# The last projection, the gate and one block of w2 change their places in the stream of a decode block

## The chip, the core and the metric

The kernel runs on one core of one Trainium2 chip. The metric is the device time of one execution in microseconds (us). Before the change it is 1055.42 us, the median of 3 runs (1055.36 to 1056.06). Smaller is better.

## The reference, cut to what matters

One token of one sequence passes through an attention with a long cache and a feed-forward part; a conditioning vector c gives six vectors that shift, scale and gate both. All is float32: D = 640, 32 heads of 192, 8192 cached positions, F = 1536.

```python
mod = (_silu(c) @ w_mod).reshape(c.shape[0], 6, 1, -1)
sa, ca, ga, sb, cb, gb = (mod[:, 0], mod[:, 1], mod[:, 2], mod[:, 3], mod[:, 4], mod[:, 5])
h = _layernorm(x, axis=-1) * (1 + ca) + sa
x = x + ga * _A_ref(h, A_k_cache, A_v_cache, A_wq, A_wo)      # softmax(q k / sqrt(192)) v, then @ wo
h = _layernorm(x, axis=-1) * (1 + cb) + sb
x = x + gb * _B_ref(h, B_w1, B_b1, B_w2, B_b2)                # relu(h w1 + b1)^2 w2 + b2
```

The two caches are 403 MB and the weights some 49 MB; each byte is used once.

## The kernel before, in words

**The stream.** All that comes from HBM is laid out by the host in the order of its use. It comes as `wm0`, 53 chunks (0 to 52) of `kv`, `wm1`, `w1`, `w2`, each with the 128 partitions as rows. All transfers are issued by SyncE (`load`, L197 to L211) and go through one queue. They land in three buffers of 16128 columns that take turns (tag "slot"): `load(n + 3)` stands at the end of the work on chunk n (L401) and waits until the buffer of chunk n is no longer read. The last chunk, `wm1`, `w1` and `w2` come in pieces, so that work can start on the first columns: the tuples `WM_CUT`, `W1_CUT`, `W2_CUT` (L43 to L45) hold the columns where a piece ends.

**A chunk** holds keys, values and, in some, a part of the query or output weights. `plan()` (L50) lays this out: (first key row, key rows, first value unit, value units, extras), an extra being ("o", pair of heads) with 1920 columns or ("q", part) with 2560. The last two chunks hold values alone. Chunk 51 holds 9 units of values and the output weights of pair 14; chunk 52 holds 7 units, in two pieces of four and three. The output weights of the last pair, 15, come at the head of `wm1`.

**Work on a chunk** (loop of L354): VectorE multiplies keys with the query (`multiply`, L249), GpSimd adds two halves of a part of the products (L376), VectorE sums (`scores`, L257), and at the end of a head the softmax follows (L268). TensorE multiplies the values (`values`, L298). After a pair of heads, `evict` (L303) and `turn` (L318) bring its output into a column, and `attend` (L324) multiplies that with the pair's part of wo and accumulates over all pairs in `att_a`.

**The end** (from L403), in program order: evict, turn and `attend` of the last pair; `mod(2, 3)`, three of the six conditioning vectors from `wm1`, with `gather` (L338) between, which brings the attention into `att_s` and spreads it; x1, layernorm, `hT2`; `gate(5)` (L424), the last conditioning vector, whose weights are the first 3200 columns of `w1`; the products with w1 (`ps_f`, L428); bias, relu and square on VectorE, then a transposition to `fT` (L431 to L434); one idle product that keeps TensorE warm (L438); the products with the 12 blocks of w2 (`ps_y`, L446); `y` and its transfer out (L451). Each engine works through its instructions in this order and waits where an operand is missing.

Of the kernel before, what the change touches and what calls it, by code (L numbers as in the profile page):

```python
# [8 lines left out]
F32 = mybir.dt.float32  # L9
# [4 lines left out]
P = 128  # L14
D = 640
H = 32
SK = 8192
DH = 192
FF = 1536
G = 4  # L20
DG = D // G
FG = FF // G
KB = DG // 32
FB = FG // 32
# [4 lines left out]
NPAIR = H // 2  # L29
NPOS = SK // P  # L30
POOL = 7
WO = 3 * D
QC = 512
NQ = H * DH // QC
RING = 3 * QC
SRING = 4 * NPOS
WQ = KB * QC
UNIT = E * DH
SLOT = 84 * DH
VPC = 5  # L40
LEAD_FROM = 1300
LEAD = 120
W1_CUT = (KB * D + 3 * FF, KB * D + KB * FF)  # L43
W2_CUT = (8 * D, 11 * D, 12 * D)
WM_CUT = (WO + 9 * D, WO + 15 * D)  # L45
WARM = 1
# [3 lines left out]
def plan():  # L50

    chunks, kp, vp, q, o = [], 0, 0, 1, 0
    while kp < H * NPOS or vp < H * NPOS // E:
        room, w = SLOT, []
        if o < NPAIR - 1 and 2 * (o + 1) * NPOS // E <= vp:
            w.append(("o", o))
            o, room = o + 1, room - WO
        used = (QC * (q - 2) - 1) // DH + 1 if q > 2 else 0
        if q < NQ and kp >= NPOS * (QC * q // DH) - 3 * NPOS // 2 and kp >= NPOS * used:
            w.append(("q", q))  # L60
            q, room = q + 1, room - WQ
        if not chunks:
            nk, nv = NPOS, 0
        else:
            v = VPC - 1 if kp >= LEAD_FROM else VPC
            nk = min(H * NPOS - kp, (room - v * UNIT) // DH)
            if kp + nk - E * (vp + v) > LEAD:
                v += 1
                nk = min(H * NPOS - kp, (room - v * UNIT) // DH)
            nv = min(H * NPOS // E - vp, (room - nk * DH) // UNIT)  # L70
            while nv and ((vp + nv - 1) // (NPOS // E) + 1) * NPOS > kp + nk:
                nv -= 1
            nk = min(H * NPOS - kp, (room - nv * UNIT) // DH)
        chunks.append((kp, nk, vp, nv, w))
        kp, vp = kp + nk, vp + nv
    assert q == NQ and o == NPAIR - 1
    return chunks


def width(chunk):  # L80
    return chunk[1] * DH + chunk[3] * UNIT + sum(WO if t == "o" else WQ for t, _ in chunk[4])


PLAN = plan()


@with_exitstack
def block_kernel(ctx: ExitStack, tc: tile.TileContext, kv, wm0, wm1, w1, w2, out):
    nc = tc.nc
    const = ctx.enter_context(tc.tile_pool(name="const", bufs=1))  # L90
# [102 lines left out]

    chunk_t = {}
    start = [sum(width(c) for c in PLAN[:n]) * P for n in range(len(PLAN))]

# [26 lines left out]
    h1 = layernorm(x_c, 1, scale_a, lambda: ma[:, :KB, 0], "ln1")  # L223
    qb = const.tile([P, RING], F32, name="qb")

# [8 lines left out]
    att_a = psum.tile([P, 512], F32, tag="att", name="att_a")  # L234
    att_s = const.tile([P, D], F32, name="att_s")
    nc.vector.memset(att_s, 0.0)
    query(0, wm0_t[:, KB * 2 * D:KB * 2 * D + WQ])
# [100 lines left out]
    def gather():  # L338

        nc.vector.tensor_copy(att_s[96:, :512], att_a[96:, :512])  # L340
        for j in range(NV):
            r = slice(32 * j, 32 * (j + 1))
            nc.scalar.activation(att_s[r, 512:], att_a[r, (D - 512) * j:(D - 512) * (j + 1)], AF.Copy)
        att_t.append(psum.tile([P, 512], F32, tag="o", name="att", bufs=3))
        for g in range(G):
            nc.tensor.matmul(att_t[0][32 * g:32 * (g + 1), :DG], sel.to_broadcast([P, 32]),
                             att_s[:, DG * g:DG * (g + 1)], start=True, stop=True)
# [6 lines left out]
    for n, (kp, nk, vp, nv, extra) in enumerate(PLAN):  # L354
# [5 lines left out]
        for what, k in extra:  # L360
            w = t[:, at:at + (WO if what == "o" else WQ)]
            at += w.shape[1]
            if what == "q":
                query(k, w)
            else:
                wo_t = (k, w)
# [29 lines left out]
        for v in range(vp, vp + nv):  # L396
            if v % (NPOS // E) == NPOS // E - 1:
                to_evict.append(v // (NPOS // E))
        if wo_t is not None:
            attend(*wo_t)  # L400
        load(n + 3)  # L401

    wm1_t, w1_t, w2_t = chunk_t["wm1_t"], chunk_t["w1_t"], chunk_t["w2_t"]  # L403
    gb_t = w1_t[:, :KB * D].rearrange("p (b n) -> p b n", b=KB)
    w1_t = w1_t[:, KB * D:KB * (FF + D)].rearrange("p (b n) -> p b n", b=KB)
    w2_t = w2_t[:, :FB * D].rearrange("p (b n) -> p b n", b=FB)

    for h in to_evict:
        evict(h)
    turn(NPAIR - 1)  # L410
    attend(NPAIR - 1, wm1_t[:, :WO])
    mod(2, 3, wm1_t[:, WO:WO + KB * 3 * D].rearrange("p (b n) -> p b n", b=KB), gather)
    x1 = const.tile([P, DG], F32, name="x1")
# [9 lines left out]

    gate(5, gb_t)  # L424
    pf = psum.tile([P, 512], F32, tag="q", name="ps_f", bufs=2)
# [8 lines left out]
    fT = columns(f, FG, "fT", work, tag="om", bufs=1)  # L434

    idle = psum.tile([P, 512], F32, tag="sm", name="ps_warm", bufs=2)
    for k in range(WARM):
# [6 lines left out]
    for b in range(FB):  # L444
        for g in range(G):
            nc.tensor.matmul(py[32 * g:32 * (g + 1), :DG], fT[:, b], w2_t[:, b, DG * g:DG * (g + 1)],  # L446
                             start=(b == 0), stop=(b == FB - 1))
# [46 lines left out]
```

## Time and profile before

| | us |
|---|---|
| median of 3 runs | 1055.42 |
| the profiled execution's own time | 1055.57 |
| its span, first to last instruction | 1053.8 |
| VectorE busy | 830.2 |
| TensorE busy (products) | 495.8 |
| GpSimd busy | 188.1 |

The span is what the profile shows; the execution's own time has 1.8 us more around it. Positions such as 1036.71 are us from the start of the span. In rows of the timeline stand the start, the duration, the engine, the line of the kernel, the operation, the tiles written and read with their shapes, the count, and in brackets the idle time before and who ended it. SPq is SyncE's queue, on which a row of a transfer is its issue; the rows of the transfers give size and us from issue to landing. Rows of a chain of waits give start, duration, what. Rows of stretches give the stretch and its length, for PE, PEld, DVE, ACT and POOL the busy us and in brackets the instructions, and then three numbers: the granted clock of TensorE (1.00 is full), the busy share of the 16 DMA engines, and GB/s.

### The profile page before, as it was taken

The page shows a single profiled execution, that of the slowest core. Times are in us where ns is not written, and L with a number is a line of the kernel's source. Part 1 is how long each engine was busy: PE and PEld are TensorE (multiplying, and loading weights), DVE is VectorE, ACT ScalarE, POOL GpSimd, SP SyncE. Part 2 cuts the span into 40 slices and gives each one's busy share as a digit, 9 for nine tenths or more (in the row PEclk, how much of TensorE's full clock was granted, in tenths as well). Part 3 has the DMA queues.
Part 4 walks back from the last instruction along what each step waited for, and adds up shares of the span by engine and source line. Part 5 has one row for each costly group of instructions (what it writes and reads, how often), then busy time and mean ns, then how long its engine had stood idle before and what let it go on. Part 6 is the DMA issues. An engine that isn't in the chain of part 4 may idle for free.

```text
span 1053.8 us, 5121 instructions
## 1 busy us (share of the span) xinstructions
PE 495.8 (47%) x2102; PEld 134.6 (13%) x2102; DVE 830.2 (79%) x428; ACT 43.4 (4%) x122; POOL 188.1 (18%) x57
## 2 busy tenths in 40 slices
PE   2153335455352363536344357344446346345286
PEld 1010011011010010101011011011011011011023
DVE  2898878877959969887797895999887977988822
ACT  1000000000000000000000000000000000000001
POOL 0212121121212202212121121122211211211200
PEclk9676576777675686668676577676777767768699
DMA  9999999999999999999999999999999999999997
GB/s 408 434 429 431 429 441 438 441 431 433 430 431 431 432 433 430 433 435 438 435 427 436 433 427 430 436 439 433 431 432 431 432 436 433 437 433 430 419 431 311
DMA packets 8959, 452.15 MB, mean 429 GB/s; under 512 B 996, under 2 KB 1000, under 8 KB 1256
## 3 DMA queue, kind: packets, MB, share of 16 engines
q1 hardware_dynamic: 8936, 451.83, 99.3%
q8 instruction: 16, 0.26, 0.1%
q14 instruction: 7, 0.06, 0.0%
HBM read 451.82 MB, written 0.00 MB: 429 GB/s over the span
## 4 chain that ended last, share of the span: by engine, by line
DMA 56%; DVE 31%; PE 11%; ACT 1%; issue 0%; SPq 0%; DVEq 0%
DMA chunk<-in_kv 53%; DVE chunk L249 16%; DVE sc L257 13%; PE ps_o L298 5%; DMA w_t<-in_w 2%; PE ps_q L230 2%; PE att_a L331 2%; DMA wm_t<-in_wm 1%; DVE os L312 1%; DVE om L310 1%; ACT p L281 0%; PE ps_mod L179 0%; PE ps_mx L273 0%; PE ps_mod L188 0%; PE att_a L333 0%
## 5 line engine op out<-in xcount | busy, mean ns | idle before, releaser
L249 DVE TENSOR_TENSOR chunk<-chunk,qb 128x8064 f32<-128x8064 f32 (+19 forms) x81 | 419.7, 5211 | 128.4 <-DMA chunk<-in_kv 123.2
L257 DVE TENSOR_REDUCE sc<-chunk 128x25 f32<-128x4800 f32 (+21 forms) x109 | 333.9, 3097 | 0.4
L298 PE MATMUL ps_o<-chunk,p 128*32 128x512 f32 x1536 | 296.7, 736 | 73.7 <-DMA chunk<-in_kv 64.3
L376 POOL TENSOR_TENSOR chunk<-chunk 128x1824 f32<-128x1824 f32 (+9 forms) x51 | 187.4, 3674 | 806.3 <-DVE chunk L249 548.4
L273 PE MATMUL ps_mx<-ident,mp 128*128 128x128 f32 x32 | 14.6, 455 | 343.9 <-DVE mp L271 343.9
L298 PEld LDWEIGHTS ps_o<-chunk,p 128*32 128x32 f32 x1536 | 67.4, 131 | 278.1 <-issue 188.1
L331 PE MATMUL att_a<-chunk,oT 128*32 128x512 f32 x90 | 63.4, 863 | 42.2 <-DVE oT L321 42.2
L230 PE MATMUL ps_q<-chunk,ln_h 128*128 128x512 f32 x110 | 66.9, 769 | 26.1 <-DMA chunk<-in_kv 26.1
L273 PEld LDWEIGHTS ps_mx<-ident,mp 128*128 128x128 f32 x32 | 5.6, 176 | 373.0 <-DVE mp L271 304.0
L281 ACT ACTIVATE p<-sc,nm 128x256 f32<-128x256 f32 x32 | 16.2, 507 | 649.9 <-DVE nm L275 649.9
L230 PEld LDWEIGHTS ps_q<-chunk,ln_h 128*128 128x128 f32 x110 | 26.5, 252 | 64.5 <-issue 35.1
L310 DVE TENSOR_TENSOR om<-ps_o,mask 96x512 f32<-96x512 f32 x32 | 21.6, 675 | 8.5 <-PE ps_o L298 8.5
L275 DVE TENSOR_REDUCE nm<-ps_mx 128x1 f32<-128x128 f32 x32 | 9.3, 292 | 19.5 <-PE ps_mx L273 19.5
L312 DVE TENSOR_REDUCE os<-om 96x64 f32<-96x512 f32 x32 | 21.8, 682 | 1.1
L331 PEld LDWEIGHTS att_a<-chunk,oT 128*32 128x32 f32 x90 | 11.7, 145 | 77.4 <-DVE oT L321 44.4
L320 DVE TENSOR_REDUCE oT<-ps_oT 128x3 f32<-128x96 f32 x16 | 4.0, 248 | 20.3 <-PE ps_oT L316 20.3
L286 PE MATMUL ps_sum<-ident,wide 128*128 128x128 f32 x16 | 7.5, 467 | 22.4 <-ACT wide L284 22.4
L179 PE MATMUL ps_mod<-wm_t,silu 128*32 128x320 f32 (+1 forms) x80 | 9.2, 608 | 15.5 <-DVE silu L167 15.5
L316 PE MATMUL ps_oT<-ident,os 96*128 96x96 f32 x16 | 5.0, 313 | 22.3 <-DVE os L312 22.3
L333 PE MATMUL att_a<-chunk,oW 128*96 128x384 f32 x30 | 14.1, 550 | 0.0
L231 ACT ACTIVATE qb<-ps_q 128x512 f32<-128x512 f32 x12 | 7.2, 597 | 136.7 <-PE ps_q L230 136.7
L329 ACT ACTIVATE oW<-oT 128x96 f32<-128x96 f32 x16 | 4.5, 280 | 177.5 <-DVE oT L321 177.5
(84 smaller groups left out, 100.9 us busy)
## 6 DMA issues: line engine op xcount, KB each, us to landing
chunk<-in_kv SPq DMA_DIRECT2D x38, 8064.0 KB, 37.5
chunk<-in_kv SPq DMA_DIRECT2D x11, 8000.0 KB, 38.3
chunk<-in_kv SPq DMA_DIRECT2D x2, 7872.0 KB, 38.5
chunk<-in_kv SPq DMA_DIRECT2D x1, 6144.0 KB, 27.6
wm_t<-in_wm SPq DMA_DIRECT2D x1, 4493.5 KB, 13.6
w_t<-in_w SPq DMA_DIRECT2D x1, 3904.0 KB, 20.7
wm_t<-in_wm SPq DMA_DIRECT2D x1, 3840.0 KB, 23.8
chunk<-in_kv SPq DMA_DIRECT2D x1, 3072.0 KB, 28.2
```

What stands on the lines that cost most here:

```text
L230: nc.tensor.matmul(ps, h1[:, b:b + 1].to_broadcast([P, P]), w[:, b], start=(b == 0), stop=(b == KB - 1))
L249: nc.vector.tensor_mul(pr, pr, q[:, None, :].to_broadcast([P, b - a, DH]))
L257: nc.vector.tensor_reduce(sc[:, a % SRING:a % SRING + b - a], src[:, a - first:b - first], axis=AX.X, op=ALU.add)
L273: nc.tensor.transpose(ps[:, :P], mp.to_broadcast([P, P]), ident)
L275: nc.vector.tensor_reduce(nm, ps[:, :P], axis=AX.X, op=ALU.max, negate=True)
L281: nc.scalar.activation(p, s[:, :, None].to_broadcast([P, NPOS, 32 // E]), AF.Exp, bias=nm, accum_out=sp[:, h % 2:h % 2 + 1])
L298: nc.tensor.matmul(ps_t[h][32 * g:32 * (g + 1)], p[:, E * j:E * (j + 1)].rearrange("p e r -> p (e r)"), t[:, g], start=(j == 0), stop=last)
L310: nc.vector.tensor_mul(om[:n], ps_t.pop(h)[:n].rearrange("p (d e) -> p d e", e=E), mask[:n, None, :].to_broadcast([n, ED, E]))
L312: nc.vector.tensor_reduce(os_[:n, h % 2], om[:n], axis=AX.X, op=ALU.add)
L331: nc.tensor.matmul(att_a[96:, :512], oT[:, j:j + 1].to_broadcast([P, 32]), w[:, j, :512], start=(first and j == 0), stop=(last and j == NV ...
L333: nc.tensor.matmul(att_a[:96, :NV * (D - 512)], oW.rearrange("p j r -> p (j r)"), w[:, :, 512:], start=first, stop=last)
L376: nc.gpsimd.tensor_add(half, half, kt[:, m:, DH // 2:])
```

## The change

The last pair's output weights go to the end of chunk 52 (its second piece), and `wm1` holds the conditioning weights alone. In `w1` the weights of the feed-forward part come first and the gate's after them, and `gate(5)` moves from before the w1 products to after `fT`. The first of the 12 blocks of w2 leaves the last transfers: it has an array `w2x` and a tile `w2x_t` of its own, and comes in two transfers, rows 0 to 124 behind the issue of chunk 23 and rows 125 to 127 behind that of chunk 24. The rest of w2 has pieces that end at columns 7 D, 11 D - 160 and 11 D. `att_s` shares the buffer of `qb`, and its memset goes from VectorE at the start to GpSimd at the end.

```diff
+EXTRA = {"o": WO, "q": WQ}
...
-W1_CUT = (KB * D + 3 * FF, KB * D + KB * FF)
-W2_CUT = (8 * D, 11 * D, 12 * D)
-WM_CUT = (WO + 9 * D, WO + 15 * D)
+W1_CUT = (3 * FF, KB * FF + KB * D)
+W2_CUT = (7 * D, 11 * D - DG, 11 * D)
+FIVE = {20: (0, 125), 21: (125, P)}
+WM_CUT = (9 * D, 15 * D)
...
     assert q == NQ and o == NPAIR - 1
+    chunks[-1][4].append(("o", NPAIR - 1))
     return chunks
...
+    w2x_t = const.tile([P, D], F32, name="w2x_t")
...
-    qb = const.tile([P, RING], F32, name="qb")
+    qb = work.tile([P, RING], F32, name="qb", tag="qb", bufs=1)
...
-    att_s = const.tile([P, D], F32, name="att_s")
-    nc.vector.memset(att_s, 0.0)
...
     def gather():
 
+        att_s = work.tile([P, D], F32, name="att_s", tag="qb", bufs=1)
+        nc.gpsimd.memset(att_s, 0.0)
...
-        if wo_t is not None:
+        if wo_t is not None and n + 1 < len(PLAN):
             attend(*wo_t)
         load(n + 3)
+        if n in FIVE:
+            a, b = FIVE[n]
+            nc.sync.dma_start(w2x_t[a:b], w2x[a:b])
...
-    gb_t = w1_t[:, :KB * D].rearrange("p (b n) -> p b n", b=KB)
-    w1_t = w1_t[:, KB * D:KB * (FF + D)].rearrange("p (b n) -> p b n", b=KB)
-    w2_t = w2_t[:, :FB * D].rearrange("p (b n) -> p b n", b=FB)
+    gb_t = w1_t[:, KB * FF:KB * (FF + D)].rearrange("p (b n) -> p b n", b=KB)
+    w1_t = w1_t[:, :KB * FF].rearrange("p (b n) -> p b n", b=KB)
+    w2_t = w2_t[:, :(FB - 1) * D].rearrange("p (b n) -> p b n", b=FB - 1)
...
     turn(NPAIR - 1)
-    attend(NPAIR - 1, wm1_t[:, :WO])
-    mod(2, 3, wm1_t[:, WO:WO + KB * 3 * D].rearrange("p (b n) -> p b n", b=KB), gather)
+    attend(*wo_t)
+    mod(2, 3, wm1_t[:, :KB * 3 * D].rearrange("p (b n) -> p b n", b=KB), gather)
...
-    gate(5, gb_t)
     pf = psum.tile([P, 512], F32, tag="q", name="ps_f", bufs=2)
...
     fT = columns(f, FG, "fT", work, tag="om", bufs=1)
 
+    gate(5, gb_t)
     idle = psum.tile([P, 512], F32, tag="sm", name="ps_warm", bufs=2)
...
-            nc.tensor.matmul(py[32 * g:32 * (g + 1), :DG], fT[:, b], w2_t[:, b, DG * g:DG * (g + 1)],
+            nc.tensor.matmul(py[32 * g:32 * (g + 1), :DG], fT[:, b], (w2_t[:, b - 1] if b else w2x_t)[:, DG * g:DG * (g + 1)],
                              start=(b == 0), stop=(b == FB - 1))
```

More of the change, by code (lines that the diff above doesn't have):

```diff
@@ L76, in plan, with block_kernel @@
     assert q == NQ and o == NPAIR - 1
+    chunks[-1][4].append(("o", NPAIR - 1))
     return chunks
 def width(chunk):
-    return chunk[1] * DH + chunk[3] * UNIT + sum(WO if t == "o" else WQ for t, _ in chunk[4])
+    return chunk[1] * DH + chunk[3] * UNIT + sum(EXTRA[t] for t, _ in chunk[4])
 PLAN = plan()
 @with_exitstack
-def block_kernel(ctx: ExitStack, tc: tile.TileContext, kv, wm0, wm1, w1, w2, out):
+def block_kernel(ctx: ExitStack, tc: tile.TileContext, kv, wm0, wm1, w1, w2, w2x, out):
     nc = tc.nc
@@ L476 @@
     kv = [np.concatenate([k[:, kp:kp + nk].reshape(P, -1), v[:, vp:vp + nv].reshape(P, -1)]
-                         + [(wo if what == "o" else wq)[i] for what, i in extra], axis=1).reshape(-1)
+                         + [{"o": wo, "q": wq}[what][i] for what, i in extra], axis=1).reshape(-1)
           for kp, nk, vp, nv, extra in PLAN]
@@ L482 @@
                                column(B_b1, FB), column(B_b2, KB)], axis=1),
-        "wm1": np.concatenate([wo[-1], rows(wm[:, 2 * D:5 * D], KB)], axis=1),
-        "w1": np.concatenate([rows(wm[:, 5 * D:], KB), rows(B_w1, KB)], axis=1),
-        "w2": rows(B_w2, FB),
+        "wm1": rows(wm[:, 2 * D:5 * D], KB),
+        "w1": np.concatenate([rows(B_w1, KB), rows(wm[:, 5 * D:], KB)], axis=1),
+        "w2": rows(B_w2, FB)[:, D:],
+        "w2x": rows(B_w2, FB)[:, :D],
     }
```

2 lines of the change are left out of this document (1 added, 1 removed).

## The prediction

> **What bounds the kernel now.** I read the page first, then the chain of waits for the last 115 us, then the timeline of the end, then stretches of the transfer rates and of the clock.
>
> ```profile
> span 1053.8 us, 5121 instructions
> PE 495.8 (47%) x2102; PEld 134.6 (13%) x2102; DVE 830.2 (79%) x428; ACT 43.4 (4%) x122; POOL 188.1 (18%) x57
> HBM read 451.82 MB, written 0.00 MB: 429 GB/s over the span
> L249 DVE TENSOR_TENSOR chunk<-chunk,qb 128x8064 f32<-128x8064 f32 (+19 forms) x81 | 419.7, 5211 | 128.4 <-DMA chunk<-in_kv 123.2
> chunk<-in_kv SPq DMA_DIRECT2D x38, 8064.0 KB, 37.5
> ```
>
> No engine is full, and VectorE waits 123 us for chunks: the stream from HBM bounds the body. A chunk of 8064 KB (8.26 MB) needs 19 us at 429 GB/s, and lands 37.5 us after its issue, so one more is always queued ahead of it. The end is another matter; the chain shows it.
>
> ```profile
> 943.04 39.25 DMA chunk<-in_kv
> 982.32 8.56 DVE chunk L249
> ...
> 1015.98 20.69 DMA w_t<-in_w
> 1036.71 4.43 PE ps_mod L188 x20
> ...
> 1046.98 3.50 PE ps_y L446 x96
> 1050.51 0.34 DVE y L449
> ```
>
> The reader is to see two anchors. The last chunk with keys lands at 982.32, and from there everything is computed work. Then the gate's weights (first piece of w1) land at 1036.71 and TensorE runs gate, w1, w2 with one break, in which VectorE makes f. Beside that chain stands the timeline:
>
> ```profile
> 982.32 8.56 DVE L249 TENSOR_TENSOR chunk<-chunk,qb 128x8064 f32<-128x8064 f32 x1 [1.36 <-DMA chunk<-in_kv]
> 1015.88 6.21 PE L298 MATMUL ps_o<-chunk,p 128*32 128x512 f32 x42
> 1024.59 2.76 PE L331 MATMUL att_a<-wm_t,oT 128*32 128x512 f32 x6 [0.68 <-DVE oT L321]
> 1027.28 0.89 PE L333 MATMUL att_a<-wm_t,oW 128*96 128x384 f32 x2
> 1037.75 0.34 DVE L122 STREAM_TRANSPOSE hT<-ln_h 128x160 f32<-128x160 f32 x1
> 1041.07 3.43 PE L428 MATMUL ps_f<-w_t,hT 128*32 128x384 f32 x40
> 1041.19 1.21 ACT L192 ACTIVATE mods<-ps_mod 32x160 f32<-32x160 f32 x4 [4.58 <-PE ps_mod L188]
> 1044.43 1.12 PE L438 MATMUL ps_warm<-w_t,ones 128*128 128x512 f32 x2
> 1046.98 3.47 PE L446 MATMUL ps_y<-w_t,fT 128*32 128x160 f32 x96 [1.43 <-DVE gb L440]
> ```
>
> hT2 is ready at 1037.75 + 0.34 = 1038.09, but TensorE is in the gate until 1041.07: the w1 products start 2.98 us late. That is what the new order can give back.
>
> **The change, part by part.** First the block of w2. The end of the stream says why a moved block isn't neutral: its share falls in a step.
>
> ```profile
> 1044.50:1045.50 1.00, 1.00 (x2) 0.22 (x2) 0.90 (x2) 0.00 (x0) 0.00 (x0) 1.00 0.81 330
> 1045.50:1046.50 1.00, 0.05 (x1) 0.00 (x0) 0.93 (x3) 0.00 (x0) 0.00 (x0) 1.00 0.59 241
> 1046.50:1047.50 1.00, 0.52 (x16) 0.55 (x20) 0.76 (x3) 0.00 (x0) 0.00 (x0) 1.00 0.52 215
> 1047.50:1048.50 1.00, 1.00 (x37) 1.00 (x32) 0.00 (x0) 0.00 (x0) 0.00 (x0) 1.00 0.48 178
> 1048.50:1049.50 1.00, 1.00 (x39) 1.00 (x32) 0.00 (x0) 0.00 (x0) 0.00 (x0) 1.00 0.10 38
> w_t<-in_w SPq DMA_DIRECT2D x1, 320.0 KB, 26.6
> 1015.98 7.44 SPq L210 DMA_DIRECT2D w_t<-in_w  x5
> ```
>
> From 1045.5 to 1048.5 the share stands near a half: about eight of the 16 DMA engines are done by 1045.3, the others work on to 1048.6. Every transfer so far gives each engine the same bytes, so I estimate that eight engines lead by 3.3 us.
>
> 125 rows can be dealt out evenly over at most 5 of 16 engines (125 = 5 x 25), 3 rows over 3. One engine runs at 178 / (0.48 x 16) = 23 to 215 / (0.52 x 16) = 26 GB/s in these rows. 25 rows of 2560 bytes are 64,000 bytes: 2.5 to 2.8 us more on five engines, in mid-stream, and nothing on the others; one of the 3 rows adds 0.1. The removed block, 320 KB over 16, was 20,480 bytes on each, 0.8 us at the very end. The Trainium skill, DMA: Bandwidth & Descriptors, section "Why a DMA increments its semaphore by 16 and not by 1", has the same dealing (the largest count up to 16 that divides the rows, on HWDGE the lowest-numbered engines), and its table of rules advises one 128-partition transfer. By that advice the block would best have stayed 0.8 us on every engine; by the step above the late ones have no time to spare and the early ones do.
>
> If the five are early ones, 3.3 - 2.7 = 0.6 us of their lead remains: no landing comes later, and the last ends at 1048.6 - 0.8 = 1047.8 instead of 1048.6. **That gain is worth nothing here**: the five issues end at 1023.42, so the last began at about 1023.0 and landed 26.6 us later, at 1049.6, and TensorE reaches its columns at about 1050.2 (the last 8 of 96 matmuls before 1046.98 + 3.47 = 1050.45). If the five are late ones, every later landing, that of 982.32 too, slips by 2.7 us. The trace has no row on who is who; the bounds are 0 and 2.7. The nearest row is the step itself: it stays flat for three us, so these are two groups and not a spread, and five neighbours are likely to lie in one of them. Which one is a judgement: I take 0, at odds of better than 2 to 1, and keep 2.7 in the range. [...]
>
> SyncE issues two transfers more behind the issues of chunks 23 and 24, at about 0.4 us; no issue waits on them, as chunks are queued 18 us ahead. Nothing waits for w2x_t before ps_y.
>
> **The last wo** moves from the head of wm1 to the tail of chunk 52. It has the same place in the byte order, but the second piece of the chunk now lands with it, 1920 columns (983,040 bytes, 2.3 us at 429 GB/s) later. Its values aren't needed until 24 of the 42 matmuls from 1015.88 are done, 3.5 us on, at 1019.4.
>
> ```profile
> 1022.14 0.33 SPq L210 DMA_DIRECT2D w_t<-in_w  x1
> w_t<-in_w SPq DMA_DIRECT2D x1, 1536.0 KB, 24.0
> ```
>
> w2 takes chunk 52's buffer, which the last attend now reads: its issue may move from 1022.14 to the end of L333, 1027.28 + 0.89 = 1028.17. Only out_y is behind it on SyncE. The second w1 piece, the second of the five issues from 1015.98 on (about 1016.4), lands at 1016.4 + 24.0 = 1040.4, so at 1028.17 the queue still holds 12 us of work: nothing. Without that cover, each us would be a us of ps_y.
>
> **att_s** takes qb's place once the last keys are multiplied (982.32 + 8.56 = 990.88), and its memset goes from VectorE's start, before any chunk's work, to GpSimd, which has nothing behind its last pair sums (18% busy); the attention is gathered after 1028. Nothing, at both ends.
>
> **The gate** goes behind w1. The first piece of w1 (3 FF, less than before) lands by 1036.71, the second, with the gate's columns last, at 1040.4. So the w1 products start with hT2 at 1038.15. From there TensorE has w1, gate and the warm-up matmul, and the f chain runs beside the gate. At full clock w1 takes 1044.43 - 1041.07 = 3.36. For the gate and for the clock:
>
> ```profile
> 1036.71:1039.81 3.10, 3.10 (x12) 1.48 (x14) 1.28 (x5) 0.00 (x0) 0.00 (x0) 0.50 1.07 451
> 1039.81:1041.07 1.26, 1.26 (x11) 0.42 (x7) 0.00 (x0) 0.00 (x0) 0.00 (x0) 1.00 0.80 342
> 22.64:26.06 3.42, 2.34 (x5) 1.22 (x6) 2.47 (x9) 0.26 (x1) 0.00 (x0) 0.50 1.03 446
> 26.06:29.47 3.41, 3.41 (x6) 1.32 (x5) 0.73 (x1) 0.00 (x0) 0.00 (x0) 0.50 0.83 358
> 1032.99:1036.40 3.41, 0.71 (x4) 0.59 (x4) 2.10 (x8) 0.06 (x1) 0.00 (x0) 1.00 0.95 406
> 1036.40:1039.81 3.41, 3.10 (x12) 1.48 (x14) 1.36 (x5) 0.20 (x1) 0.00 (x0) 0.50 1.09 458
> ```
>
> The gate did 3.10 us at half clock and 1.26 at full: 1.55 + 1.26 = 2.81 at full clock. The warm-up is two matmuls of 512; six such took 2.76, so 0.92. Sum: 1038.15 + 3.36 + 2.81 + 0.92 = 1045.24 at full clock, and half of the time at half clock comes on top. The clock changes in steps of 3.41 us; a step busy for 2.34 was followed by another half-clock step, one busy for 3.10 by full clock. After the change TensorE idles longer, until 1038.15, so it starts at half clock. With this run's steps (1039.81, 1043.23) the first step is busy for 1.66 only, and half clock lasts to 1043.23: 5.08 us, price 2.54. With steps that lie otherwise it lasts 2.4 to 6.5 us, price 1.2 to 3.2; the middle is 2.2. ps_y then starts at 1047.4 (1046.4 to 1048.4) instead of 1046.98. The f chain isn't later: w1 wholly at half clock ends at 1038.15 + 6.7 = 1044.9, and 2.5 us on (as from 1044.43 to 1046.98) is 1047.4. The gate's four copies (1.21 us in all) and gb2 come after the gate and end by 1049, before y needs them at 1050.51 or later.
>
> So **2.98 us of early start are spent**: 2.81 + 0.92 now stand between w1 and w2, where before the 2.5 us of f stood with the warm-up inside, and 0.6 more on the cold clock. Sum: 0 (block) + 0 (wo, w2's issue, att_s) + 0.4 = 1054.2 of span. The profiled execution took 1055.57 beside its span of 1053.8, 1.8 around it, and lies 0.15 above the median of 1055.42. 1055.57 + 0.4 - 0.15 = **1055.8**.
>
> **Rivals.**
> 1. *The five are late engines* (slower). The chunk of 982.32 lands 2.7 us later, and all to the end is chained to it; VectorE's 1.36 us of idle before it only grow. 1055.8 + 2.7 = 1058.5. It decides when the lead of the slowest of the five is under 2.7 us. For it: half of the engines are late, and one late one among the five is enough. Against: the flat step, by which the five are hardly mixed.
> 2. *Foreign partitions cost double.* Five engines then write the partitions that 16 share; were two writers to halve each other, 25 rows would take 5.4 us, 3.3 are covered, and 2.1 reach 982.32: 1057.9. No row shows two writers on one partition group. The Trainium skill, SBUF — State Buffer, section "Door 1: The DMA port swizzle", would have it so: bandwidth depends on the ports that the partitions reach, and rows 0 to 24 lie on seven ports of other engines' traffic.
> 3. *The clock comes back early*: price 1.2 instead of 2.2 and ps_y at 1046.4: 1054.8. It takes steps that start right with w1.
> 4. *The change doesn't do what it says*: 125 rows go through one engine. 320,000 bytes at 26 GB/s are 12.3 us, 3.3 covered: 1055.8 + 9 = 1064.8. For it: nothing but an odd count.
>
> **How the numbers follow.** Forecast 0.52, rival 1 0.20, rival 2 0.15, rival 3 0.10, rival 4 0.03. The range takes in rival 3 with some margin and rivals 1 and 2: 1054.4 to 1058.6; the forecast's own part is 1055.0 to 1056.8. A measurement of this kernel tells about 0.2% (2.1 us) from no change, so slower begins at 1057.5: rival 4, most of 1 and over half of 2 make 0.27. No case is faster by 2.1 us; 0.04 is left for what I don't see, 0.69 for the same.
>
> **What would show it.** w1's products start within 0.2 us of hT2, gate and warm-up fill the f chain, ps_y waits for TensorE and no longer for VectorE: right. The wait for the last chunk with keys stays near 982: the five are early; at 985: rival 1 or 2, and a share above a half that ends in mid-stream tells between them. The stream's share at the end drops later and more steeply, and ends by 1048. Wrong: ps_y starting before 1046, or a stall inside it for w2's last piece.

## The result, and the profile after

The changed kernel is slower, by 0.44%. Beside each other on one chip it took 1060.64 us (median of 6 runs, 1060.23 to 1061.94) and the kernel before 1055.80 (6 runs, 1055.36 to 1057.11): a ratio of 1.0044, interval 1.0033 to 1.0055, or 4.8 us. The forecast of 1055.8 and the range up to 1058.6 both missed it. The profiled execution took 1060.57 beside a span of 1058.8, before 1055.57 beside 1053.8: the span is 5.0 longer, and what lies around it is 1.8 again.

Lines on the change's path have moved: L249 is L251 (multiply), L298 is L300 (values), L331 and L333 are L333 and L335 (attend), L210 is L214 (load), L446 is L453 (w2 products). First the page of the changed kernel.

```profile
span 1058.8 us, 5124 instructions
HBM read 451.82 MB, written 0.00 MB: 427 GB/s over the span
L251 DVE TENSOR_TENSOR chunk<-chunk,qb 128x8064 f32<-128x8064 f32 (+19 forms) x81 | 419.7, 5212 | 131.7 <-DMA chunk<-in_kv 126.0
```

The same bytes come at 427 instead of 429 GB/s, the multiplies take exactly as long as before, and VectorE waits 2.8 us more for chunks (126.0 against 123.2). The work has not grown; the stream has lost time. The chain of waits (start, duration, what) says where it is lost:

```profile
946.73 39.26 DMA chunk<-in_kv
986.01 8.56 DVE chunk L251
...
1027.90 4.20 PE att_a L333 x6
...
1051.91 3.47 PE ps_y L453 x96
```

The last chunk with keys sets the end again, but its multiply starts at 986.01 instead of 982.32: 3.69 us of the 5.0 are there before any instruction of the new end has run. The timelines of both kernels show where they arise. Before:

```profile
467.79 9.03 DVE L249 TENSOR_TENSOR chunk<-chunk,qb 128x6528 f32<-128x6528 f32 x2 [1.82 <-DMA chunk<-in_kv]
486.69 4.16 DVE L249 TENSOR_TENSOR chunk<-chunk,qb 128x3840 f32<-128x3840 f32 x1
```

After, with the issues that matter and the end:

```profile
432.47 0.36 SPq L408 DMA_DIRECT2D w2x_t<-in_w2x  x1
468.93 9.03 DVE L251 TENSOR_TENSOR chunk<-chunk,qb 128x6528 f32<-128x6528 f32 x2 [3.04 <-DMA chunk<-in_kv]
490.88 4.16 DVE L251 TENSOR_TENSOR chunk<-chunk,qb 128x3840 f32<-128x3840 f32 x1 [3.01 <-DMA chunk<-in_kv]
...
1019.29 15.14 SPq L214 DMA_DIRECT2D w_t<-in_w  x5
1027.90 4.20 PE L333 MATMUL att_a<-chunk,oT 128*32 128x512 f32 x6 [0.68 <-DVE oT L323]
1042.70 0.34 DVE L125 STREAM_TRANSPOSE hT<-ln_h 128x160 f32<-128x160 f32 x1
1043.10 4.91 PE L434 MATMUL ps_f<-w_t,hT 128*32 128x384 f32 x40 [1.85 <-DVE hT L125]
1047.94 2.91 PE L191 MATMUL ps_mod<-w_t,silu 128*64 128x320 f32 x20
1050.79 1.13 PE L445 MATMUL ps_warm<-w_t,ones 128*128 128x512 f32 x2
1051.84 0.48 PE L453 MATMUL ps_y<-w2x_t,fT 128*32 128x160 f32 x8
```

The 125 rows are issued at 432.47 and begin to move 32 us later, behind chunk 23 and ahead of chunk 24. Chunk 23, the one ahead of them, is multiplied 1.14 us late (468.93), chunk 24, the one behind them, 4.19 us late (490.88), and there VectorE now waits 3.01 us where before it waited for nothing. The stretches of the transfer rates at this place are, before (the last two numbers are the DMA share and GB/s):

```profile
465.00:466.00 1.00, 0.47 (x1) 0.18 (x1) 0.33 (x2) 0.00 (x0) 0.00 (x0) 0.50 0.74 320
470.00:471.00 1.00, 1.00 (x9) 0.34 (x6) 1.00 (x1) 0.00 (x0) 0.00 (x0) 0.50 0.44 192
```

and after, here and at the end of the stream:

```profile
465.00:466.00 1.00, 0.47 (x1) 0.18 (x1) 0.29 (x1) 0.07 (x1) 0.00 (x0) 0.50 0.43 131
466.00:467.00 1.00, 0.08 (x1) 0.08 (x1) 0.00 (x0) 0.84 (x3) 0.00 (x0) 0.50 0.73 192
469.00:470.00 1.00, 1.00 (x9) 0.30 (x6) 1.00 (x1) 0.00 (x0) 0.00 (x0) 0.50 0.67 218
...
1048.00:1049.00 1.00, 1.00 (x12) 0.57 (x10) 0.88 (x2) 0.00 (x0) 0.00 (x0) 1.00 0.76 321
1049.00:1050.00 1.00, 1.00 (x10) 0.55 (x8) 0.93 (x3) 0.00 (x0) 0.00 (x0) 1.00 0.38 142
1050.00:1051.00 1.00, 1.00 (x9) 0.38 (x6) 0.25 (x1) 0.10 (x1) 0.00 (x0) 1.00 0.08 33
```

The share alone jumps about in both, since packets are long; the quotient tells more. A full share brings 320/0.74 = 432 and 192/0.44 = 436 GB/s before, but 131/0.43 = 305, 192/0.73 = 263 and 218/0.67 = 325 after: the engines are busy and move less.

The packet records of the trace, one packet for each row of a transfer, give the same from nearer by:

```
                           rows    mean     beside them, rows of about 64 KB
one transfer of 128 rows   128     103 ns   longest 2393 ns
the change, 125 rows       125     161 ns   longest 3621 ns, 23.8 us over 2385 ns in all
(rows of the first kind from the run e1_one128 below)
```

In the change the five engines begin their rows at 464.90, 465.17, 465.42, 465.56 and **467.40**: four are ahead, one is 2 us behind them. That one ends at 471.27, so its 25 rows took 3.87 us instead of 25 x 0.103 = 2.58.

The records tell too when a chunk is complete. Behind a transfer each engine that took part writes a packet of 4 bytes: there are 16 of them behind a chunk, five more behind the 125 rows and three behind the 3. The last of the 16 completes the chunk. For chunk 23 it ends at 468.08, 0.7 us after the late one of the five began its rows. From chunk 22 complete to chunk 24 complete the kernel before takes 37.95 us and the change 42.22, so **the block costs 4.27 us at its place**. Behind it the delay doesn't stay the same: against the kernel before it is 4.2 us up to chunk 31, 2.6 to 2.9 from chunk 32 to 37 and 3.6 from chunk 38 on. The 3.69 at the last chunk with keys is what later steps of the landings have left of it.

At the end, 4.86 us are to be accounted for at the start of the w2 products (1051.84 against 1046.98): 3.69 from the last chunk with keys, less 0.38 won in the values between, 1.44 because TensorE's clock fell to half within the last attend (granted 0.64 from 1027.90 to 1032.10, before 1.00; 4.20 us instead of 2.76) with 0.20 on what follows it, which makes hT2 at 1043.04 4.95 late, and -0.09 from hT2 to the w2 products (8.80 against 8.89). The new order at the end, by itself, is neutral in this execution.

### The profile page after: what moved, and what is told of

Read it like the earlier page. It is cut to its first block, busy times and chain, and to the rows that moved or that the text cites. A ratio compares the mean times of both kernels' runs of the same rounds, so it can differ in the third digit from the quotient of the medians.

```text
span 1058.8 us, 5124 instructions
## 1 busy us (share of the span) xinstructions
PE 490.8 (46%) x2102; PEld 133.1 (13%) x2102; DVE 829.9 (78%) x427; ACT 43.5 (4%) x122; POOL 188.6 (18%) x58
## 4 chain that ended last, share of the span: by engine, by line
DMA 54%; DVE 32%; PE 13%; ACT 1%; issue 0%; SPq 0%; DVEq 0%
DMA chunk<-in_kv 53%; DVE chunk L251 16%; DVE sc L259 13%; PE ps_o L300 5%; PE att_a L333 2%; PE ps_q L234 2%; DMA wm_t<-in_wm 1%; PE ps_mod L182 1%; DVE os L314 1%; DVE om L312 1%; PE att_a L335 0%; PE ps_f L434 0%; ACT p L283 0%; PE ps_mx L275 0%; PE ps_y L453 0%
## 5 line engine op out<-in xcount | busy, mean ns | idle before, releaser
L251 DVE TENSOR_TENSOR chunk<-chunk,qb 128x8064 f32<-128x8064 f32 (+19 forms) x81 | 419.7, 5212 | 131.7 <-DMA chunk<-in_kv 126.0
L300 PE MATMUL ps_o<-chunk,p 128*32 128x512 f32 x1536 | 295.1, 732 | 75.8 <-DMA chunk<-in_kv 66.3
L300 PEld LDWEIGHTS ps_o<-chunk,p 128*32 128x32 f32 x1536 | 67.0, 130 | 279.5 <-issue 187.5
L333 PE MATMUL att_a<-chunk,oT 128*32 128x512 f32 x96 | 64.9, 831 | 43.0 <-DVE oT L323 43.0
L333 PEld LDWEIGHTS att_a<-chunk,oT 128*32 128x32 f32 x96 | 12.1, 142 | 79.0 <-DVE oT L323 45.4
L335 PE MATMUL att_a<-chunk,oW 128*96 128x384 f32 x32 | 15.0, 550 | 0.0
L331 ACT ACTIVATE oW<-oT 128x96 f32<-128x96 f32 x16 | 4.5, 280 | 177.0 <-DVE oT L323 177.0
```

What stands on the lines that cost most here:

```text
L251: nc.vector.tensor_mul(pr, pr, q[:, None, :].to_broadcast([P, b - a, DH]))
L300: nc.tensor.matmul(ps_t[h][32 * g:32 * (g + 1)], p[:, E * j:E * (j + 1)].rearrange("p e r -> p (e r)"), t[:, g], start=(j == 0), stop=last)
L333: nc.tensor.matmul(att_a[96:, :512], oT[:, j:j + 1].to_broadcast([P, 32]), w[:, j, :512], start=(first and j == 0), stop=(last and j == NV ...
L335: nc.tensor.matmul(att_a[:96, :NV * (D - 512)], oW.rearrange("p j r -> p (j r)"), w[:, :, 512:], start=first, stop=last)
```

## The experiments

All medians stand beside the kernel before on the same chip, 1056.08 us for the first five, 1056.14 for e4, e6, e7 and e8, 1056.31 for the others. **The lateness of a chunk** is the start of its multiply against the same row of the kernel it is compared with.

A position late in the stream scatters: in the profiles of e2, e8, e12 and e13, which have no block in the stream, the last chunk with keys is complete 0.32, -0.05, 0.62 and -0.61 us later than in the kernel before. So beside it stands the **price at the place**: the time from chunk 22 complete to chunk 24 complete in the packet records, less the 37.95 us of the kernel before.

```
                                                    rows       price at the place, us
e2, e8, e12, e13                                    none       0.00
e1; also e10, e11, e14, e15, ahead of added rows    128        0.83
e4                                                  64 + 64    2.39
e3                                                  125 + 3    4.05
the change                                          125 + 3    4.27
e5                                                  124 + 4    5.45
```

### One transfer of 128 rows: e1

```diff
-FIVE = {20: (0, 125), 21: (125, P)}
+FIVE = {20: (0, P)}
```

> The block of w2 comes in one transfer of 128 rows at the same place (16 engines, 20,480 bytes each); all else as in the changed kernel, in which the last chunk with keys starts to be multiplied at 986.01, 3.69 us later than before. Theory A (the dealing of 125 rows over five engines costs it, by late engines among them or by foreign partitions): the chunk starts 0.8 us later than before, near 983, and the time falls by about 3 us, to 1057.5. Rival B (a further transfer in the middle of the stream costs it, whatever its rows): the chunk stays near 986, the time near 1060.6.

1057.58 us, 1.0017 (1.0008 to 1.0025). The timeline:

```profile
467.60 9.03 DVE L251 TENSOR_TENSOR chunk<-chunk,qb 128x6528 f32<-128x6528 f32 x2 [1.84 <-DMA chunk<-in_kv]
487.30 4.16 DVE L251 TENSOR_TENSOR chunk<-chunk,qb 128x3840 f32<-128x3840 f32 x1 [0.77 <-DMA chunk<-in_kv]
982.79 8.56 DVE L251 TENSOR_TENSOR chunk<-chunk,qb 128x8064 f32<-128x8064 f32 x1 [1.43 <-DMA chunk<-in_kv]
```

The same bytes at the same place, dealt to all 16 engines, cost 0.83 us there instead of 4.27. (At the last chunk with keys it is 0.47 instead of 3.69, 982.79 against 982.32, but 0.47 is within the scatter.) So it is the shape of the transfer that costs, not that w2's block lies in the middle. Moving it is still not free: these bytes stood behind all chunks before and stand ahead of 29 of them now, 0.8 us by their size.

### The end alone and the block alone: e2, e3

e2 keeps the new end and leaves the block in w2:

```diff
-W2_CUT = (7 * D, 11 * D - DG, 11 * D)
-FIVE = {20: (0, 125), 21: (125, P)}
+W2_CUT = (8 * D, 12 * D - DG, 12 * D)
...
-    w2x_t = const.tile([P, D], F32, name="w2x_t")
```

> The new end without the block: block 0 of w2 stays in the last transfers, no w2x. Theory A (the block costs nearly all): last chunk with keys at 982 to 982.5, time within 1 us of the kernel before (1055.8 beside it), a little above for the half clock in front of w1. Rival C (the end itself costs 1.2 of the 4.8 us, since TensorE meets the last wo at half clock: 4.20 us for six matmuls instead of 2.76): 1057 and the same 4.2 us in this profile.

1056.92 us, 1.0009 (1.0000 to 1.0018). The timeline of TensorE:

```profile
1025.70 2.76 PE L331 MATMUL att_a<-chunk,oT 128*32 128x512 f32 x6 [0.68 <-DVE oT L321]
1039.27 6.30 PE L429 MATMUL ps_f<-w_t,hT 128*32 128x384 f32 x40 [1.85 <-DVE hT L124]
1045.50 2.91 PE L190 MATMUL ps_mod<-w_t,silu 128*64 128x320 f32 x20
1049.39 3.47 PE L448 MATMUL ps_y<-w_t,fT 128*32 128x160 f32 x96
```

The attend from chunk 52 takes 2.76, as before: the 4.20 of the change belong to where the clock's steps fell, not to the new place of the last wo. The w1 products start with hT2, nearly all at half clock (granted 0.50 up to 1042 and 0.56 from there to 1045.57; 6.30 instead of 3.43, a price of 2.87). The profiled execution took 1058.01, 1.1 above the median, so this price is one of the high ones.

e3 is the opposite, the old end with the block in 125 and 3 rows:

```diff
-W2_CUT = (8 * D, 11 * D, 12 * D)
+W2_CUT = (7 * D, 10 * D, 11 * D)
+FIVE = {20: (0, 125), 21: (125, P)}
...
+        if n in FIVE:
+            a, b = FIVE[n]
+            nc.sync.dma_start(w2x_t[a:b], w2x[a:b])
```

> The end as before (wo of the last pair in wm1, gate ahead of w1, w1's pieces as before), with the block in transfers of 125 and 3 rows and att_s in qb's place. Theory A: last chunk with keys 3.7 us later than before, time 1055.8 + 3.7 = 1059.5. If the end costs a part of its own (rival C) it is the rest of the 4.8. If the end is what is slow: 1056.

1060.27 us, 1.0040 (1.0026 to 1.0053). The timeline:

```profile
985.98 8.56 DVE L250 TENSOR_TENSOR chunk<-chunk,qb 128x8064 f32<-128x8064 f32 x1 [1.36 <-DMA chunk<-in_kv]
1041.41 5.42 PE L190 MATMUL ps_mod<-w_t,silu 128*64 128x320 f32 x20 [1.64 <-DMA w_t<-in_w]
```

The last chunk with keys is at 985.98, 3.66 us late, as in the change. The block alone makes 4.2 of the 4.8 us, the end alone 0.8, with an interval from none to 1.9. In e3 the gate waits for its weights until 1041.41, so the lost time of the stream reaches that landing too.

### Four engines: e5

```diff
-FIVE = {20: (0, 125), 21: (125, P)}
+FIVE = {20: (0, 124), 21: (124, P)}
```

> 124 rows and 4 rows instead of 125 and 3: 124 = 4 x 31, so four engines of 31 rows. In the changed kernel four of the five engines that got the 25 rows began on them at 464.9 to 465.6 and one at 467.4, that is four early engines and one late one. Theory A1 (the late engine among the five is what shows; rows are slower but covered): if it is the fifth, it is free now, and the chunk after the block starts within 2 us of before although each engine has more rows (31 x 0.17 = 5.3 us, 2.5 to 3 covered). If it is one of the first four: 31 rows instead of 25, so 0.9 to 1.0 us more than the changed kernel. Theory A2 (foreign partitions slow all engines alike, who is late doesn't matter): as the changed kernel, +4.2 us after the block.

1061.75 us, 1.0053 (1.0039 to 1.0067). The timeline:

```profile
467.89 9.03 DVE L251 TENSOR_TENSOR chunk<-chunk,qb 128x6528 f32<-128x6528 f32 x2 [2.40 <-DMA chunk<-in_kv]
491.67 4.16 DVE L251 TENSOR_TENSOR chunk<-chunk,qb 128x3840 f32<-128x3840 f32 x1 [4.84 <-DMA chunk<-in_kv]
986.89 8.56 DVE L251 TENSOR_TENSOR chunk<-chunk,qb 128x8064 f32<-128x8064 f32 x1 [1.36 <-DMA chunk<-in_kv]
```

Four engines with 31 rows each are worse than five with 25, by 0.8 us at the multiply (491.67 against 490.88) and by 1.2 at the place. Six rows more take 0.6 us at 103 ns and 0.9 at 157. In the packet records the four begin at 465.08, 465.50, 465.55 and 466.98, and the last of them is here the last of all 16 to end chunk 23, where the late one of the change had 0.7 us in hand. So a late engine is among these four as well, and the six rows with the missing 0.7 us, 1.3 to 1.6 by this estimate, come near the 1.2.

### Same bytes on every engine, half the partitions: e4

On top of e1:

```diff
-FIVE = {20: (0, P)}
+FIVE = {20: ((0, 64), (64, P))}
...
-            a, b = FIVE[n]
-            nc.sync.dma_start(w2x_t[a:b], w2x[a:b])
+            for a, b in FIVE[n]:
+                nc.sync.dma_start(w2x_t[a:b], w2x[a:b])
```

> The block in two transfers of 64 rows at the same place instead of one of 128. Every engine gets 4 + 4 rows, as many bytes as with 128 rows; what differs is the partitions: with 128 rows the 16 engines write 16 groups of eight, with 64 rows all 16 write the partitions of one half. Theory P (a partition group takes about one engine's rate): two engines share a group, rows of 2560 bytes take near 200 ns instead of 103, the block takes 1.6 us instead of 0.8 and the chunk behind it comes 0.8 us later than with 128 rows. Theory D (only the number of rows for each engine counts): rows 103 ns, chunk and time as with 128 rows.

1059.37 us, 1.0031 (1.0019 to 1.0043), against e1's 1.0017 (1.0008 to 1.0025). The timeline:

```profile
468.73 9.03 DVE L251 TENSOR_TENSOR chunk<-chunk,qb 128x6528 f32<-128x6528 f32 x2 [3.18 <-DMA chunk<-in_kv]
488.69 4.16 DVE L251 TENSOR_TENSOR chunk<-chunk,qb 128x3840 f32<-128x3840 f32 x1 [1.03 <-DMA chunk<-in_kv]
984.30 8.56 DVE L251 TENSOR_TENSOR chunk<-chunk,qb 128x8064 f32<-128x8064 f32 x1 [1.36 <-DMA chunk<-in_kv]
```

Each engine moves eight rows, as in e1, but 16 engines write 64 partitions at a time, and the last chunk with keys is 1.51 us later than in e1 (984.30 against 982.79); at the place it is 1.56. The packet records say how: the rows take 159 ns instead of 103, and the 64-KB rows beside them 17.8 us more in all. Spread over 16 engines that is (128 x 0.055 + 17.8)/16 = 1.55 us. No engine has more to do here, so this is the price of **who writes which partitions**, apart from who is late. That there are two transfers instead of one isn't the reason: e10 and e14 (below) add four at a place and lose nothing at the first two places.

### The same engines, own and foreign partitions: e6, e7, then e10, e11, e14, e15

All six are e1 and load a few rows of the block again, into the same place, in transfers of 5 rows. As before, five engines take one row each. In "own" the rows lie below partition 64, on partitions that, as the expectation has it, these five engines write anyway; in "foreign" they lie at 64 and above. The bytes on the five engines are the same in a pair. e6 and e7 add eight transfers at each of three places, which makes 40 rows loaded again each time:

```diff
+        if n in (23, 26, 29):
+            for h in (0, 32):        # e7: (64, 96)
+                for o in range(4):
+                    nc.sync.dma_start(w2x_t[h + o:h + o + 20:4], w2x[h + o:h + o + 20:4])
```

> The block in one transfer of 128 rows, and at three places (behind chunks 26, 29 and 32) 40 of its rows once more, in eight transfers of five rows each, four partitions apart from partition 0 and 32 on (0, 4, 8, 12, 16 and so on). So five engines get 8 x 2560 bytes more at each place, and each writes to the group of partitions that it writes in a transfer of 128 rows. Theory P: no sharing, rows near 103 ns, 0.8 us at each place, which shows only as far as a late engine is among the five: 0 to 0.8 us for each place. Theory D: the same. A rule by which few rows are slow as such: rows of 160 ns here too.

> As the run before, the same five engines, the same number of rows and transfers, but partitions 64, 68, 72, 76, 80 and so on and from 96 on, which other engines are writing meanwhile. Theory P: rows of 160 to 200 ns, 1.3 to 1.6 us on the five engines, and 0.8 us of delay for the owners of these groups too; the chunks behind the three places come up to 2 us later in all than in the run before. Theory D: as the run before, rows near 103 ns.

1070.60 us, 1.0137 (1.0121 to 1.0153), and 1071.84, 1.0147 (1.0133 to 1.0161). Both miss their purpose. The timeline of SyncE in e6:

```profile
486.43 40.24 SPq L409 DMA_DIRECT2D w2x_t<-in_w2x  x8
526.78 17.30 SPq L214 DMA_DIRECT2D chunk<-in_kv  x3
```

and its stretch:

```profile
526.00:527.00 1.00, 1.00 (x6) 0.19 (x3) 0.98 (x1) 0.00 (x0) 0.00 (x0) 0.50 0.00 0
```

Eight small issues in a row hold SyncE for 40.24 us, since it waits for earlier transfers to land (in the whole run these issues wait 102.6 us for chunks); the next chunk is issued only at 526.78, and the stream has run dry at 526. What they cost is this stall, and the pair tells nothing of partitions. With four transfers at each place (20 rows loaded again) SyncE doesn't stall. e10 and e11 have three places, e14 and e15 six:

```diff
+        if n in (23, 26, 29):        # e14, e15: (23, 26, 29, 32, 35, 38)
+            for o in range(0, 4):    # e11, e15: range(64, 68)
+                nc.sync.dma_start(w2x_t[o:o + 20:4], w2x[o:o + 20:4])
```

> As the run with own partitions, with four transfers of five rows at each of the three places instead of eight (partitions 0, 4, 8, 12, 16 and the three sets beside them), since eight had SyncE wait for a semaphore and the queue ran dry. Five engines get 4 x 2560 bytes more at each place, on the groups that they write anyway. Theory P: rows near 103 ns while the other engines stream; the chunks behind the places slip by 0 to 0.5 us each. Rival (few rows are slow as such): rows of 150 to 180 ns.

> The same with partitions 64, 68, 72, 76, 80 and the three sets beside them, which other engines are writing. Theory P: rows of 150 to 200 ns as in the changed kernel, and the rows of 64 kB that the owners write beside them stretch by 0.4 us in all at each place. Theory D (only bytes for each engine count): as with own partitions.

> Own partitions at six places instead of three: 24 rows more in all on each of the five engines, nearly the 25 of the change, with no foreign partition. If the five engines' own lateness makes up the loss of the change: 24 x 0.103 = 2.5 us, less what the last of the five had in hand (0.9 us by its place among the 16 before the block), so chunks 1.6 us later than with the one transfer of 128 rows, and if none of the five is late, nothing.

> The same six places with foreign partitions: 24 rows on each of the five engines. If the partitions carry the larger part: as at three places per place, 0.7 to 1.0 us each, 4.5 to 6 us in all against the transfer of 128 rows, and 3 us or more above the own partitions.

```
                       median    ratio (interval)           rows     last chunk with keys, later than e1
e10 own, 12 rows       1058.21   1.0019 (1.0008 to 1.0029)  103 ns   0.83
e11 foreign, 12 rows   1060.26   1.0041 (1.0025 to 1.0056)  118 ns   3.05
e14 own, 24 rows       1058.72   1.0025 (1.0014 to 1.0035)  103 ns   1.87
e15 foreign, 24 rows   1062.85   1.0063 (1.0046 to 1.0080)  119 ns   5.31
(rows: on each of the five engines; ns: mean of one row in the packet records)
```

The last column comes from the timelines, 982.79 of e1 against, in this order,

```profile
983.62 8.56 DVE L251 TENSOR_TENSOR chunk<-chunk,qb 128x8064 f32<-128x8064 f32 x1 [1.36 <-DMA chunk<-in_kv]
```

```profile
985.84 8.56 DVE L251 TENSOR_TENSOR chunk<-chunk,qb 128x8064 f32<-128x8064 f32 x1 [1.36 <-DMA chunk<-in_kv]
```

```profile
984.66 8.56 DVE L251 TENSOR_TENSOR chunk<-chunk,qb 128x8064 f32<-128x8064 f32 x1 [1.36 <-DMA chunk<-in_kv]
```

```profile
988.10 8.56 DVE L251 TENSOR_TENSOR chunk<-chunk,qb 128x8064 f32<-128x8064 f32 x1 [1.37 <-DMA chunk<-in_kv]
```

That column holds scatter too: of e10's 0.83, 0.68 is there at chunk 22, ahead of the first added row. So the places themselves, as for the block: how much longer than in the kernel before it takes from the chunk ahead of the place complete to the chunk behind it complete.

```
added rows stand behind    chunk 26   chunk 29   chunk 41
e1, none added               0.00       0.01       0.00
e10 own                      0.00       0.00       none added
e14 own                      0.00       0.01       0.41
e11 foreign                  0.69       0.72       none added
e15 foreign                  0.67       0.72       1.02
(us; each place adds 4 rows, 0.41 us at 103 ns, on each of the five. The places behind
chunks 32, 35 and 38 are left out: there runs without added rows step by up to 1.3 us)
```

"Own" is the lateness of the five engines by itself. At the first place the slowest of them has 0.9 us in hand: it begins its added rows at 524.68 in e10 and 524.73 in e14, and the last of the 16 ends the chunk at 525.59 and 525.64. The 0.82 us of two places are covered by that, and nothing arrives. At the place behind chunk 41 it is itself the last of the 16, and all of the 0.41 arrives. So the slowest of the five leads by 0.9 us, not by 3.3. "Foreign" costs 0.7 us at each of the first two places, at equal bytes per engine: there the owners of those partitions are held up too (8 us of stretched 64-KB rows at each place, against under 0.6 for own).

### Could the new end be made to pay? e8, e12, e13

The clock eats what the early start of w1 gives. So e8 and e12 keep TensorE awake in the second layernorm, with idle products, on top of e2 (and leave out the warm-up product behind the gate); e13 does so in the kernel before, and keeps its warm-up product.

```diff
+    def fill(n):
+        for k in range(n):
+            nc.tensor.matmul(idle, ones, wm1_t[:, 512 * k:512 * (k + 1)], start=True, stop=True)
...
+        fill(2)        # before the sum of the mean;     e8: 4
...
+        fill(1)        # before the sum of the variance; e8: 2
...
+        fill(2)        # behind it;                      e8: 4
```

> The new end without the block (block 0 stays in the last transfers), with ten idle matmuls of 512 columns in the gaps of the second layernorm and none behind the gate: TensorE should meet w1 at full clock. Theory of the sum: w1 3.4 and gate 2.9 us at full clock from hT2 on, ps_y 6.5 us after hT2 instead of 8.8 to 9.3; it then waits for the last piece of w2 near 1049.6, and y is 0.5 to 1 us earlier than before: 1055.2 beside 1055.8, against 1056.7 for the end alone. Rival: the idle matmuls delay the small products of the layernorm by 0.4 us each and nothing is gained.

1057.01 us, 1.0009 (1.0000 to 1.0018). The fill was twice too long. The timeline:

```profile
1033.18 3.70 PE L431 MATMUL ps_warm<-wm_t,ones 128*128 128x512 f32 x8
1036.72 0.28 PE L139 MATMUL ps_ln_tm<-ln_s,ones 128*128 128x1 f32 x2
1042.41 3.43 PE L438 MATMUL ps_f<-w_t,hT 128*32 128x384 f32 x40
```

Four idle products are eight instructions and 3.70 us, and the layernorm's own sums queue behind them. The w1 products run at full clock (3.43) but start at 1042.41.

> The end alone with five idle matmuls instead of ten (2, 1 and 2): one takes 0.86 us at full clock, not 0.43 as the run before had it, and there they held the layernorm up by 2.4 us. Now they fit the gaps of 1.9, 1.0 and 1.8 us. w1 starts within 0.5 us of hT2 at full clock, ps_y some 6.5 us after hT2 and then waits for the last piece of w2 at about 1049.6; y starts near 1050.0: 1055.4 for the time, against 1056.9 for the end alone and 1056.1 before. Rival: the stream ends later than I think and the time is that of before.

1056.25 us, 1.0000 (0.9991 to 1.0009). The timeline of the half-sized fill:

```profile
1039.25 3.43 PE L438 MATMUL ps_f<-w_t,hT 128*32 128x384 f32 x40
1042.61 2.91 PE L193 MATMUL ps_mod<-w_t,silu 128*64 128x320 f32 x20
1044.33 0.58 DVE L124 STREAM_TRANSPOSE fT<-f 128x384 f32<-128x384 f32 x1
1046.81 0.33 DVE L448 TENSOR_TENSOR gb<-mods,bbt 128x160 f32<-128x160 f32 x1 [1.91 <-ACT mods L197]
1047.23 2.38 PE L454 MATMUL ps_y<-w_t,fT 128*32 128x160 f32 x64 [1.71 <-DVE gb L448]
1050.06 1.29 PE L454 MATMUL ps_y<-w_t,fT 128*32 128x160 f32 x32 [0.44 <-DMA w_t<-in_w]
```

Now w1 starts at once and at full clock, and the w2 products stop for the last piece of w2 until 1050.06. What holds the w2 products until 1047.23 isn't f, which is ready at 1044.91. The profile names VectorE's gb, which ends at 1047.14, behind ScalarE's copies of the gate; the landing of w2's first piece, which holds the same products in e13 until 1046.76, may be what counts here too, and the record doesn't settle it. So with a warm TensorE the new end is bound by one of these and then by the landing of w2's last piece, and it gains nothing over the kernel before.

> The kernel before with the same five idle matmuls in the layernorm and its own one behind w1. The gate should run at full clock (2.9 us instead of 4.4), w1 be done 1.5 us earlier, ps_y start near 1045.4 instead of 1047.0 and wait for the last 320 KB of w2 at 1049.6, of which it still has 8 matmuls to do: y near 1050.1, 0.4 us earlier; 1055.7 beside 1056.1. Rival: TensorE's idle matmuls delay the gate, which waits for its weights at 1036.7, and nothing is gained.

1055.85 us, 0.9996 (0.9988 to 1.0005): no gain that can be told. The timeline:

```profile
1046.76 3.52 PE L454 MATMUL ps_y<-w_t,fT 128*32 128x160 f32 x96 [2.12 <-DMA w_t<-in_w]
```

Gate and w1 end earlier, and the w2 products then wait for w2's landing up to 1046.76. No version here is measurably faster than the kernel before.

## Why the prediction was wrong, point by point

**The block: forecast 0, measured 4.1 to 4.3 at its place, with 3.7 of it left at the last chunk with keys.** This is the step that failed: that the five lie in one group of engines, the early one, and that its lead of 3.3 us covers their 2.7 with 0.6 to spare. The flat half share at the end was rightly read as two groups; in the change the 16 engines end chunk 22 in two as well, nine from 445.84 to 446.51 and seven from 447.34 to 448.17. But the five are mixed: four begin their rows at 464.9 to 465.6 and one at 467.40. And a lead read from a few stretches at the end was given to each of them in the middle of the stream, where the slowest of the five had 0.7 us in hand (the change) to 0.9 (e10 and e14). The size was short too: 2.5 to 2.8 us for 25 rows, which took 3.87 on the late engine. The chunk waits for the last of 16 engines: one late engine among five is as bad as five, as rival 1 said, at a chance of 0.20.

**Rivals 1 and 2 were not alternatives.** Each was priced as if the other didn't hold: 2.7 us for late engines, 2.1 for foreign partitions, and the latter with 3.3 us covered. Both act, and what is not covered by the one is not covered by the other. An estimate: 25 rows at 103 ns, 2.6 us, less the 0.7 in hand, make 1.9 of lateness; the foreign partitions of e4 make 1.6 (2.39 less 0.83); together 3.5, where 4.1 to 4.3 were measured at the place. That sum carries e4's price over to another shape and falls short by 0.6 to 0.8, so the division is argued and a rest stays open. That both parts exist is shown (e14's place behind chunk 41 for the one, e4 and the first two places of the pairs for the other). Rival 2 also had the wrong payer: it doubled the time of the five alone, while the profile shows their rows at 161 instead of 103 ns (less than double) and the owners' 64-KB rows at up to 3621 ns. The range ended at 1058.6 because no case in it let both happen. 125 rows over a single engine (rival 4) is not seen: five engines begin them.

The Trainium skill, SBUF — State Buffer, section "Door 1: The DMA port swizzle (why `[64,N]` ≈ `[32,N]`)", ties the bandwidth to the ports that the partitions reach, by which 64 neighbouring partitions have half of them. e4's 159 instead of 103 ns agree, and so do the pairs: partitions from 64 on lie on other ports than those below. The Trainium skill, DMA: Bandwidth & Descriptors, section "🎯 Rules for kernel authors", advises one 128-partition transfer instead of two for disjoint halves; e1 against e4 bears it out, at 1.5 us.

**The removed 0.8 us at the stream's end are worth nothing here:** right. The share falls more steeply, as foretold (0.76, 0.38, 0.08 from 1048 on), but ends at about 1050 and not by 1048, since all is late. That w2's landing isn't far off either is shown by e12, where it ends the products' wait at 1050.06.

**The last wo, w2's issue and att_s: 0**, right. The five issues now last until 1019.29 + 15.14 = 1034.43, as the buffer comes free after the last attend, and no product of the change waits for w2. The attend from chunk 52 takes its 2.76 us in e2.

**The gate behind w1: forecast +0.4.** The mechanism was right: w1 within 0.1 us of hT2 in e2, in the change and in e12; in the first two gate and warm-up are back to back behind it, and w2 is bound by TensorE and not by f. The end alone (e2) measured +0.8, from none to 1.9. From hT2 to the w2 products the forecast had 1047.4 - 1038.09 = 9.3 us; e2 took 10.18 (1039.21 to 1049.39), the change 8.80. Both lie in the band of cold prices, 1.2 to 3.2: 2.87 in e2, 4.91 - 3.43 = 1.48 in the change. What it left out is that the clock's steps can fall badly ahead of hT2 as well: 1.44 us at the last attend. Rival 3, the clock back early, is near what the change had at w1, and it gave nothing as the attend had paid for it. One sentence of the prediction doesn't add up: the 2.98 us of early start aren't spent by 3.73 - 2.5 of work and 0.6 of cold clock, 1.8 in all. The gate's old half clock lay ahead of w1, so all of the 2.2 is new between w1 and w2, and 1.2 + 2.2 = 3.4 is what the forecast's 1047.4 holds.

## What to carry to other kernels

In a saturated stream a transfer should use all engines and all partitions: one of 320 KB cost 0.8 us at its place over 128 rows and 4.1 to 4.3 over 125 and 3, at the same bytes. A consumer waits for the last engine, so before giving some engines more work, find the lead of the slowest of them at that place, and not the mean lead at the end. When two rivals load the same resource, price them together too: the range has to hold their sum. And a small price is read between two landings around the place, which agree to 0.01 us in runs without a block, and not at one position late in the stream, which scatters by 0.6.

## What the hardware showed that was not expected

- **Writers on foreign partitions slow the owners**, and by more than themselves: in the change the 125 rows lost 125 x 58 ns = 7 us of engine time, the 64-KB rows beside them 24 us. Four rows on each of five engines cost 0.7 us on foreign partitions and nothing on own ones (first two places of the pairs).
- **Engines of one queue drift apart**, under equal bytes: in the kernel before, the first and the last of the 16 are 1.1 us apart at the end of `wm0`, 2.6 at chunk 22 and 4.1 at chunk 50. The packet records hold 16 packets of 16 KB for instructions (queue q8), of 1.0 to 1.2 us each, between the data's, and the distance grows from 2.6 to 3.9 within chunk 32, in which one of them falls (623.9). They are the likeliest reason, but that they fall on some engines only was inferred from gaps between packets and not tried. Which of the engines is the late one stays open, too, as the records carry no number of the engine.
- **Eight small issues in a row on SyncE stalled for 40 us** (e6), four did not.
- **Half clock can last through nearly all of 6.30 us of busy products** (e2), and the same products took 4.91 in the change: about 1.4 us either way for one piece of work, by where the steps fall.
